# Routing on VectorE in fewer pieces, thresholds as values, and w1 laid out in load order, in an attention and mixture-of-experts kernel

## Chip, cores and metric

The kernel runs on one core of a Trainium2 chip. The metric is the device time of one execution in microseconds (us). Lower is better.

## What is computed

Two layers in one program. The first is an attention with a squared Relu in place of a softmax, over 8 batches of 2496 rows of 256 columns. Its result x, 19968 rows, goes to a mixture of 8 experts with a capacity of 2496 rows each. All (row, expert) pairs are taken in order of falling logit; a row goes to the first expert that still has room. Then each expert's two layers run over its rows.

```python
scores = (1.0 / S) * np.matmul(z, z.transpose(0, 2, 1))
x = (u * np.matmul(np.maximum(scores, 0.0) ** 2, v)).reshape(B * S, D)
logits = x @ w_gate
for idx in np.argsort(-logits.flatten()):
    tok, e = idx // E, idx % E
    if assigned[tok] >= 0 or counts[e] >= cap:   # cap = N // E = 2496
        continue
    assigned[tok] = e
    counts[e] += 1
for e in range(E):
    mask = assigned == e
    out[mask] = np.maximum(x[mask] @ w1[e], 0.0) @ w2[e]   # w1: 256 x 1024, w2: 1024 x 256
```

## The kernel before, in words

**Stages.** Up to about 1358 us the attention runs; all its large matmuls are in pieces of a high and a low part (`hi`, `lo`). Up to about 1423 us there is almost nothing but the routing of the first expert to be filled. From then on the experts run, one after the other, PE nearly always busy, with the routing of the next expert beside them on VectorE (DVE).

**Order of the work.** The attention has an order written out by hand for PE, ScalarE (ACT) and DVE, and so has the first group of the first expert (`first_group`). Everything else is traced in program order and put into each engine's queue by a planner, which uses durations of its own; each engine then works through its queue in order. `advance` mixes the steps of `route(k + 1)` into the loop over expert k, in proportion to the numbers that the generator yields. `behind(lag)` and `issue_after` hold some routing steps behind a step of the expert on the same engine. `warm` puts matmuls without a use into PE's queue while route 0 is alone.

**route(k)** finds the k-th expert that gets full. It has these parts:
- For k > 0 the closed expert is taken out of the logits `lg` (L338), each row's best remaining expert is found by `best_expert` in four quarters of 40 columns (L80 to L97: maximum, comparison, code, one-hot `oh`), and `order_keys` (L108 to L118) turns the maximum into an integer key, a copy `rep` of its upper half eight times over, and `top` and `low`, the halves as floats.
- A search for a threshold in two stages (upper half, lower half), of 5 rounds in route 0 and 6 in the others, each settling 2 to 4 bits. A round makes n = 3, 7 or 15 thresholds `T` from the last digit `Dg` and a prepared row `W` = step + base `V` (L379), compares all keys (`at_least`, L124, `mask`), counts per expert by matmuls (`hist` L281, or `quad_hist` L303 and `quad_sums` L313, L317 in route 0), and takes the largest step that still leaves an expert full (L410, L415). `V` (L394) and the next `W` (L401) are made behind the mask. At the end of a stage `tstar` = `V` + `Dg` (L417).
- Ranks by running sums, and the list: a row's place in its expert's list is split into two digits, one-hot forms of both are made (`oa` L514, `ob` L523 in four pieces for each of four column blocks), `oa` is multiplied by the two halves of the row's number (`hl`, L517), and matmuls add up the list (L529). Route 0 does this in two parts of its own (L541, L554, L559, L564).

**Weights.** `load_w` loads w1 and w2 of the expert in halves, `split_w` makes the high part on ACT (L618) and the low part on DVE (L621). For w1 the source is read with a stride of four elements (L612), for w2 without.

**Experts.** `layer1` makes the first layer for 128 hidden columns and 512 rows (L672 to L674; `hp`, two banks), Relu on ACT (L750, `hh`) and its low part on DVE (L752, `hl_`; L755 for the last 64 rows of an expert). `layer2` (L768, L770) adds up the result three steps behind; `put_y` adds the two halves (L793) and scatters. `gather_x`, `tip_x`, `split_x` fetch and turn the rows of the next group. GpSimd issues gathers and scatters, and prepares `slot` and `hq` (L256, L294) when the attention has ended.

Of the kernel before, what the change touches and what calls it, by code (L numbers as in the profile page):

```python
# [22 lines left out]
def tile_attention_then_moe(ctx, tc, u, ut, v, z, w_gate, gate_rows, w1, w2, out):  # L23
# [36 lines left out]
                 at0=consts.tile([128, 15], I16, name="at0"),  # L60
                 mask0=consts.tile([128, JP, 15], BF, name="mask0"))
    at0_f = consts.tile([128, 15], F32, name="at0_f")
    nc.gpsimd.iota(at0_f, pattern=[[1, 15]], base=1, channel_multiplier=0, allow_small_or_imprecise_dtypes=True)
# [41 lines left out]
def key_steps(nc, first, c, alone):  # L105
# [7 lines left out]
    n = half.shape[1]  # L113
# [22 lines left out]
def moe(tc, xd, first, jp, identf, w1, w2, out, B, S, cp, dram):  # L136
# [19 lines left out]
    ND = 15  # L156
    LA = 3
# [3 lines left out]
    with ExitStack() as ctx:  # L161
# [21 lines left out]
        nc.vector.memset(ones16, 1.0)  # L183
# [27 lines left out]
        need = const([128, E, 16], F16, "need")  # L211
        nc.vector.tensor_scalar(need, dN[:, :, None].to_broadcast([128, E, 16]), float(cap), None, op0=OP.mult)

        floor = const([128, 1], F32, "floor")
        nc.vector.memset(floor, -32768.0)

        def search_plan(i, widths):
            n = max((1 << w) - 1 for w in widths)
            step = const([128, len(widths), n], F32, f"step{i}")
            sh = 16  # L220
            for r, w in enumerate(widths):
# [7 lines left out]
            n = (1 << widths[0]) - 1  # L229
            at0 = const([128, n], I16, f"at0{i}")  # L230
            nc.vector.tensor_scalar(at0, step[:, 0, :n], -32768.0, None, op0=OP.add)
            n = (1 << widths[1]) - 1
            next0 = const([128, n], F32, f"next0{i}")
            nc.vector.tensor_scalar(next0, step[:, 1, :n], -32768.0, None, op0=OP.add)
            return widths, step, at0, next0
# [5 lines left out]
                       base=0, channel_multiplier=1)  # L241
        nc.gpsimd.iota(idi[:TL, B * NT:J], pattern=[[2 * S, B // 2]], base=NT * 128, channel_multiplier=1)
        nc.gpsimd.iota(idi[TL:, B * NT:J], pattern=[[2 * S, B // 2]], base=S + NT * 128, channel_multiplier=1)
# [5 lines left out]
        nc.vector.tensor_scalar(idh_i, idi, 127, None, op0=OP.bitwise_and)  # L249
        nc.vector.tensor_copy(idl, idh_i)  # L250
# [4 lines left out]
        slot = rp.tile([128, 128, QW], BF, name="slot")  # L255
# [19 lines left out]
        nc.vector.tensor_copy(hx, ones_j[:, :1].to_broadcast([128, E * (ND + 1)]).rearrange("p (e t) -> p e t", e=E))  # L275

        def hist(masks, n, order):
            p = srch()
            for c in range(NC):
                lo, of = [s for s in masks if s[0] <= c * 16][-1]  # L280
                latest["mm"] = nc.tensor.matmul(p[:, :n * 16], oh[:, c * 16:(c + 1) * 16].rearrange("p j e -> p (j e)"),  # L281
                                                of(slice(c * 16 - lo, c * 16 - lo + 16)), start=(c == 0),
                                                stop=(c == NC - 1))
# [5 lines left out]
            nc.vector.tensor_mul(hx[:, :, :n], r[:, None, :n].to_broadcast([128, E, n]),  # L289
                                 dE[:, :, None].to_broadcast([128, E, n]))  # L290
            return hx, n + n % 2

        hq = rp.tile([128, 4 * E * (ND + 1)], F16, name="hq")
        nc.gpsimd.tensor_copy(hq, ones_j[:, :1].to_broadcast([128, 4 * E * (ND + 1)]))  # L294

        def quad_hist(of, n, r):
            o = ps.tile([128, 512], F32, name=f"y{r % 2}", bufs=1)[:, :E * (n + n % 2)]
            nc.tensor.matmul(o, ones16, need[:, :, :n + n % 2], start=True, stop=False)
# [9 lines left out]
        def quad_sums(p, o, n, order):  # L308
            nn = n + n % 2
            x = hq[:, :4 * E * nn]  # L310
            v = p[:, :4 * n]
            v = v.rearrange("p (t j) -> p j t", t=n) if order == "tj" else v.rearrange("p (j t) -> p j t", t=n)
            nc.vector.tensor_tensor(x.rearrange("p (j e t) -> p j e t", j=4, e=E)[:, :, :, :n],  # L313
                                    v[:, :, None].to_broadcast([128, 4, E, n]),
                                    own[:, :, :, None].to_broadcast([128, 4, E, n]), op=OP.mult)
            for j in range(4):
                nc.tensor.matmul(o, ones16, x[:, j * E * nn:(j + 1) * E * nn], start=False, stop=(j == 3))  # L317
# [14 lines left out]
        def route(k):  # L332
            if k:
# [29 lines left out]
            else:  # L363
# [6 lines left out]
                widths, step, at0, next0 = plans[k > 0]  # L370
                for stage in range(2):
                    V = floor
                    for r, w in enumerate(widths):
# [6 lines left out]
                        mask = []  # L380
# [4 lines left out]
                        mask.append((0, lambda j, t=whole, n=n: t[:, j, :n]))  # L385
                        yield 2
                        if k:
                            x, nn = hist(mask, n, "jt")
                        else:
                            p, o = quad_hist(mask[0][1], n, r)  # L390
                        warm(k, 4)
                        if r:
# [916 lines left out]
```

## Time and profile before

| | us |
|---|---|
| median of 3 runs | 2431.34 (2430.28 to 2432.57) |
| the profiled execution | 2432.56 |
| its span, first to last instruction | 2430.5 |

| engine | busy us | share | instructions |
|---|---|---|---|
| TensorE (PE), matmuls | 2380.0 | 98% | 14724 |
| VectorE (DVE) | 2068.5 | 85% | 6220 |
| ScalarE (ACT) | 1521.4 | 63% | 2890 |
| GpSimd (POOL) | 460.6 | 19% | 690 |

A share is an average over stages with different limits; what counts for an edit is who is waited for in the stage where it stands. Matmul ends are modelled, and matmuls made by `warm` count as busy. The granted clock is the share of TensorE's full speed that the chip gave.

### The profile page before, as it was taken

What the parts mean: (1) busy time and instruction counts of PE and PEld (TensorE: products, weight loads), DVE (VectorE), ACT (ScalarE), POOL (GpSimd) and SP (SyncE); (2) the same over time, 40 slices, a digit from 0 to 9 for tenths busy, and PEclk for the clock granted to TensorE, in tenths of its full rate; (3) what the DMA queues carried; (4) which work ended last, traced back from release to release, by engine and by line L of the source; (5) the groups of instructions that cost most, each with busy time, mean ns of one, the idle gap of its engine ahead of it and who ended that gap; (6) DMA issues with size and microseconds to landing.
All of it is one profiled execution on the core that took longest, in us unless ns stands there. A gap on an engine that the chain in (4) does not pass through costs nothing.

```text
span 2430.5 us, 42677 instructions
## 1 busy us (share of the span) xinstructions
PE 2380.0 (98%) x14724; PEld 1983.2 (82%) x14724; DVE 2068.5 (85%) x6220; ACT 1521.4 (63%) x2890; POOL 460.6 (19%) x690
## 2 busy tenths in 40 slices
PE   8999999999999999999999999899999999999998
PEld 6888888888888888888887787787888888888887
DVE  7898998998999998989989798979797979797443
ACT  7888888888888988888888223333332333333332
POOL 3020020020010200200100022333233333333332
PEclk9999999999999999999999999999999999999999
DMA  5153261261251532611511023232323323243331
GB/s 154 43 148 86 57 160 43 58 176 53 71 145 44 138 95 57 159 43 53 137 53 43 10 66 118 78 109 80 115 87 95 111 84 118 78 124 119 98 96 57
DMA packets 233848, 222.28 MB, mean 91 GB/s; under 512 B 95392, under 2 KB 192672, under 8 KB 233504
## 3 DMA queue, kind: packets, MB, share of 16 engines
q1 hardware_dynamic: 193088, 150.58, 21.3%
q0 software_dynamic: 40544, 68.98, 10.5%
q8 instruction: 116, 1.90, 0.3%
q14 instruction: 100, 0.82, 0.1%
HBM read 158.67 MB, written 60.82 MB: 90 GB/s over the span
## 4 chain that ended last, share of the span: by engine, by line
PE 82%; DVE 10%; issue 4%; POOL 1%; ACT 1%; DMA 1%; POOLq 0%; DVEq 0%; SPq 0%; ACTq 0%
PE acc L1038 41%; PE sc L996 11%; PE y L768 8%; PE hp L672 4%; PE hp L674 4%; PE hp L673 4%; PE y L770 4%; PE srch L281 2%; PE acc L1043 1%; POOL xg L590 1%; DVE mask L124 1%; DVE ob L523 1%; DVE w1l L621 1%; PE xp L325 1%; PE srch L529 1%
## 5 line engine op out<-in xcount | busy, mean ns | idle before, releaser
L1025 DVE TENSOR_TENSOR lo<-r,hi 128x512 fp32r<-128x512 f32 (+1 forms) x800 | 536.1, 673 | 83.1 <-ACT hi L1017 80.1
L1038 PE MATMUL acc<-hi,vh 128*128 128x512 f32 (+1 forms) x1520 | 590.8, 389 | 0.2 <-ACT vh L970 0.2
L1038 PE MATMUL acc<-lo,vh 128*128 128x512 f32 (+1 forms) x1520 | 587.7, 387 | 2.7 <-DVE lo L1025 2.7
L1038 PE MATMUL acc<-hi,vl 128*128 128x512 f32 (+1 forms) x1520 | 585.9, 385 | 0.0
L750 ACT ACTIVATE hh<-hp 128x512 fp32r<-128x512 f32 (+1 forms) x319 | 187.3, 587 | 629.9 <-PE hp L674 518.4
L1017 ACT ACTIVATE hi<-r 128x512 fp32r<-128x512 f32 (+1 forms) x780 | 500.2, 641 | 122.1 <-ACT r L1012 87.0
L1012 ACT ACTIVATE r<-r 128x512 f32<-128x512 f32 (+1 forms) x800 | 503.6, 639 | 2.5 <-DVE r L1006 2.4
L1079 DVE SCALAR_TENSOR_TENSOR lt<-xs,wgb 128x256 bf16<-128x256 f32 x1192 | 449.2, 417 | 0.0
L768 PE MATMUL y<-w,hh 128*128 128x512 f32 x1216 | 444.8, 399 | 0.7 <-DVE y L793 0.7
L1038 PEld LDWEIGHTS acc<-hi,vh 128*128 128x128 f32 x1520 | 286.2, 188 | 67.0 <-issue 13.8
L1008 ACT ACTIVATE r<-sc 128x512 f32<-128x512 f32 (+1 forms) x638 | 312.4, 614 | 40.3 <-PE sc L996 39.7
L1038 PEld LDWEIGHTS acc<-lo,vh 128*128 128x128 f32 x1520 | 286.3, 188 | 59.2 <-DVE lo L1025 8.2
L1038 PEld LDWEIGHTS acc<-hi,vl 128*128 128x128 f32 x1520 | 286.3, 188 | 52.1
L590 POOL DMA_INDIRECT xg<-xd,idx x160 | 181.2, 1133 | 513.3 <-DVE xg L628 281.1
L768 PEld LDWEIGHTS y<-w,hh 128*128 128x128 f32 x1216 | 229.0, 189 | 49.0 <-DVE y L793 2.2
L672 PE MATMUL hp<-xh,w1h 128*128 128x512 f32 (+2 forms) x642 | 256.5, 400 | 3.6 <-DVE hh L755 2.7
L673 PE MATMUL hp<-xl,w1h 128*128 128x512 f32 (+2 forms) x642 | 252.5, 393 | 1.2 <-DVE xl L666 1.1
L674 PE MATMUL hp<-xh,w1l 128*128 128x512 f32 (+2 forms) x642 | 250.6, 390 | 0.0
L996 PE MATMUL sc<-z,z 64*128 64x512 f32 (+1 forms) x1920 | 236.9, 389 | 4.2 <-ACT z L961 2.8
L996 PEld LDWEIGHTS sc<-z,z 64*128 64x128 f32 x1920 | 200.7, 185 | 31.2 <-ACT z L961 3.5
L959 POOL DMA_DIRECT2D z<-in_z_dram x35 | 18.7, 534 | 960.0 <-DVE lt L1079 530.0
L801 POOL DMA_INDIRECT out_dram<-y,idx x160 | 160.4, 1003 | 207.8 <-DVE y L793 120.9
(1193 smaller groups left out, 3152.1 us busy)
## 6 DMA issues: line engine op xcount, KB each, us to landing
ur<-in_u_dram SPq DMA_DIRECT2D x39, 512.0 KB
flat<-tr SPq DMA_DIRECT2D x152, 128.0 KB
xt<-flat SPq DMA_DIRECT2D x38, 512.0 KB
vh<-in_v_dram POOLq DMA_DIRECT2D x133, 128.0 KB
vr<-in_v_dram SPq DMA_DIRECT2D x32, 512.0 KB
xd<-tr SPq DMA_DIRECT2D x128, 128.0 KB
xs<-xd SPq DMA_DIRECT2D x32, 512.0 KB
wr<-in_moe_w_dram SPq DMA_DIRECT2D x32, 512.0 KB
```

The lines of the kernel that those rows point to most:

```text
L590: return nc.gpsimd.indirect_dma_start(out=dst, out_offset=None, in_=src, in_offset=bass.IndirectOffsetOnAxis(ap=idx, axis=0))
L672: nc.tensor.matmul(p[:, c], wh, xh, start=(d == 0), stop=False)
L673: nc.tensor.matmul(p[:, c], wh, xl, start=False, stop=False)
L674: latest["mm"] = nc.tensor.matmul(p[:, c], wl, xh, start=False, stop=(d == DH - 1))
L768: nc.tensor.matmul(o, h[:, c], w.rearrange("p s d -> p (s d)"), start=(f == 0), stop=(f == FT - 1), skip_group_check=True)
L996: nc.tensor.matmul(pair[s], key[b, p][r, c * 128:c * 128 + 128], query[b, g][r, :w], start=key is ZH and query is ZH, stop=key is ZL)
L1008: recent["r"] = nc.scalar.activation(r, p, AF.Relu, scale=scale)
L1012: nc.scalar.activation(R[n], R[n], AF.Square)
L1017: nc.scalar.activation(h, R[n], AF.Copy)
L1025: recent["l"] = nc.vector.tensor_sub(LO[n], a, h.bitcast(F32))
L1038: nc.tensor.matmul(o[d], w[:, c[d]], x, start=(kt == 0 and i == 0), stop=False)
L1079: nc.vector.scalar_tensor_tensor(t[r], src[r], 1.0, WG["rows"][r, e], op0=OP.mult, op1=OP.mult, accum_out=lg[r, j, e:e + 1])
```

## The change

It does the following.
- Thresholds: counts are scaled by 2^17 (`UNIT`), so that `min(count - capacity, 0) + T` is the threshold itself where an expert is still full and something lower where not. The largest of these is the new base `V`. `T` of the next round is `step + V`, one column wider (its last entry is the base). `W`, `Dg`, `tstar`, `floor` and `next0` go.
- `best_expert` in two halves of 80 columns instead of four quarters.
- `ob` in two pieces for each column block instead of four.
- The rows' numbers are split into 64s and the partition's index instead of 128s and a remainder, in float16 instead of bfloat16; the low part of `hl` is then a product with one scalar per partition, done on ACT.
- `top` and `low` are made on ACT where all keys are made at once (routes 1 to 7).
- w1 is stored in the order in which `split_w` reads it, so that L612's stride is gone.
- GpSimd clears `hq` and the `step` rows (memset); `hx` is cleared on DVE.

```diff
     spread(nc, rep, half[:, :, 1], alone)
     yield
+    if half.shape[1] == first["key"].shape[1]:
+        nc.scalar.activation(top, half[:, :, 1], AF.Copy, scale=65536.0)
+        nc.scalar.activation(low, half[:, :, 0], AF.Copy)
+        return
...
-        idh = const([128, JP], BF, "idh")
-        idl = const([128, JP], BF, "idl")
-        nc.vector.tensor_scalar(idh_i, idi, 7, None, op0=OP.logical_shift_right)
+        idh = const([128, JP], F16, "idh")
+        idl = const([128, JP], F16, "idl")
+        nc.vector.tensor_scalar(idh_i, idi, 6, None, op0=OP.logical_shift_right)
...
-        nc.vector.tensor_copy(idl, idh_i)
+        nc.vector.tensor_copy(idl, pcol.to_broadcast([128, JP]))
...
-        nc.gpsimd.tensor_copy(hq, ones_j[:, :1].to_broadcast([128, 4 * E * (ND + 1)]))
+        nc.gpsimd.memset(hq, 0.0)
...
-                for c in range(0, JP, JP // 4):
-                    eq = rp.tile([128, JP // 4, E], BF, name="eq")
-                    best_expert(nc, first, slice(c, c + JP // 4), eq)
+                for c in range(0, JP, JP // 2):
+                    eq = rp.tile([128, JP // 2, E], BF, name="eq")
+                    for i, _ in enumerate(best_steps(nc, first, slice(c, c + JP // 2), eq)):
+                        if i == 2:
+                            yield 6.8 / 4
                     yield 6.8 / 4
...
-                            T = rp.tile([128, ND], I16, name="T", bufs=2)
-                            nc.vector.tensor_tensor(T[:, :n], W[:, :n], Dg.to_broadcast([128, n]), op=OP.add)
+                            T = rp.tile([128, ND + 1], I16, name="T", bufs=2)[:, :n + 1]
+                            nc.vector.tensor_tensor(T, step[:, r, :n + 1], V.to_broadcast([128, n + 1]), op=OP.add)
...
-                        if r:
-                            V2 = rp.tile([128, 1], F32, name="V", bufs=2)
-                            nc.vector.tensor_tensor(V2, V, Dg, op=OP.add)
-                            V = V2
-                        if r == 0:
-                            W = next0
-                        elif r + 1 < len(widths):
-                            W = rp.tile([128, ND], F32, name="W", bufs=2)
-                            n2 = (1 << widths[r + 1]) - 1
-                            nc.vector.tensor_tensor(W[:, :n2], step[:, r + 1, :n2], V.to_broadcast([128, n2]), op=OP.add)
...
-                                                       o.rearrange("p (e t) -> p e t", e=E)[:, :, :n], 0.0,
-                                                       step[:, r, None, :n].to_broadcast([128, E, n]),
-                                                       op0=OP.is_ge, op1=OP.mult)
-                        Dg = rp.tile([128, 1], F32, name="Dg", bufs=2)
-                        nc.vector.tensor_reduce(Dg, best[:, :, :n], axis=AX.XY, op=OP.max)
-                    tstar = rp.tile([128, 1], F32, name="tstar")
-                    nc.vector.tensor_tensor(tstar, V, Dg, op=OP.add)
+                        best = rp.tile([128, E, ND + 1], F32, name="best")[:, :, :n + 1]
+                        nc.vector.scalar_tensor_tensor(best, o.rearrange("p (e t) -> p e t", e=E), 0.0,
+                                                       T[:, None].to_broadcast([128, E, n + 1]),
+                                                       op0=OP.min, op1=OP.add)
+                        V = rp.tile([128, 1], F32, name="V", bufs=3)
+                        nc.vector.tensor_reduce(V, best, axis=AX.XY, op=OP.max)
+                    tstar = V
...
-                    for i, d in enumerate((idh, idl)):
-                        nc.vector.tensor_mul(hl[:, :, i], oa, by_quad(d[:, q], KT))
+                    nc.vector.tensor_mul(hl[:, :, 0], oa, by_quad(idh[:, q], KT))
+                    nc.scalar.activation(hl[:, :, 1], oa, AF.Copy, scale=pcol)
                     yield 1.5
-                    for b in range(0, 128, 32):
-                        z = b + 32
+                    for b in range(0, 128, 64):
+                        z = b + 64
...
-                        yield 1.5
+                        yield 3
...
-                src = src.rearrange("p (h m q) -> p h q m", h=DH, q=FT // 2)[:, half]
+                src = src.rearrange("p (h q m) -> p h q m", h=DH, q=FT // 2)[:, half]
...
+    w1 = _blocks(inputs['moe_w1'], 1)
+    e, _, f = w1.shape
+    laid['moe_w1'] = w1.reshape(e, d, 2, 128, f // 256).swapaxes(3, 4).reshape(w1.shape)
```

## Rows read from the trace of the kernel before

**Rows 1.** The page, busy time of the engines.

```profile
PE 2380.0 (98%) x14724; PEld 1983.2 (82%) x14724; DVE 2068.5 (85%) x6220; ACT 1521.4 (63%) x2890; POOL 460.6 (19%) x690
```

**Rows 2.** Stretches of 10 us: busy PE, PEld, DVE, ACT, POOL; granted clock, DMA share, GB/s.

```profile
1530.00:1540.00 10.00, 6.25 (x98) 5.25 (x96) 10.00 (x18) 2.34 (x6) 0.00 (x0) 1.00 0.01 2
1540.00:1550.00 10.00, 9.10 (x33) 7.91 (x34) 10.00 (x32) 2.61 (x3) 7.67 (x7) 0.66 0.25 79
...
1680.00:1690.00 10.00, 9.80 (x58) 8.52 (x57) 8.81 (x30) 3.39 (x7) 1.26 (x2) 0.83 0.16 52
...
2060.00:2070.00 10.00, 10.00 (x54) 8.36 (x53) 8.61 (x26) 3.71 (x7) 2.70 (x3) 0.89 0.19 66
```

**Rows 3.** PE's waits, 1500 to 2200 us (last row 1820 to 1945): total, times, longest.

```profile
PE srch L281 <- DVE mask L124: 9.8, 5, 3.3
PE hp L672 <- DVE hh L755: 2.7, 1, 2.7
PE y L770 <- DVE hl__29448 L752: 2.0, 1, 2.0
PE srch L529 <- DVE ob L523: 1.9, 1, 1.9
...
PE srch L281 <- DVE mask L124: 1.9, 1, 1.9
```

**Rows 4.** Timeline of DVE and PE at a first mask: start, us, instruction, idle before.

```profile
1678.35 0.23 DVE L116 TENSOR_SCALAR top<-key 128x160 f32<-128x160 int16 x1
1678.50 0.23 DVE L118 CAST low<-key 128x160 f32<-128x160 int16 x1
...
1680.20 1.09 PE L281 MATMUL srch<-mask,oh 128*128 128x112 bf16 x10 [3.32 <-DVE mask L124]
```

**Rows 5.** DVE's groups by line and shape, from 1420 us: busy us, mean ns of one.

```profile
L523 DVE TENSOR_TENSOR ob<-rab,slot 128x1280 bf16<-128x1280 bf16 x112 | 88.1, 815 | 0.0
L621 DVE TENSOR_TENSOR w1l<-wr,w1h 128x512 fp32r<-128x512 f32 x30 | 32.2, 1079 | 1.0 <-PE hp L674 1.0
L621 DVE TENSOR_TENSOR w<-wr,w 128x512 fp32r<-128x512 f32 x32 | 21.9, 688 | 0.6 <-ACT w L618 0.6
...
L517 DVE TENSOR_TENSOR hl<-oa,idl 128x800 bf16<-128x800 bf16 x28 | 15.8, 566 | 0.0
L514 DVE TENSOR_TENSOR oa<-rab,slot 128x800 bf16<-128x800 bf16 x28 | 15.7, 560 | 0.0
...
L394 DVE TENSOR_TENSOR V<-V,Dg 128x1 f32<-128x1 f32 x48 | 7.3, 153 | 0.0
```

**Rows 6.** Timeline of DVE in the search of route 0.

```profile
1370.25 0.17 DVE L379 TENSOR_TENSOR T<-W,Dg 128x7 int16<-128x7 f32 x1
1370.34 0.15 DVE L394 TENSOR_TENSOR V<-V,Dg 128x1 f32<-128x1 f32 x1
1370.45 0.89 DVE L124 TENSOR_TENSOR mask<-rep,T 128x560 bf16<-128x560 int16 x2
...
1378.61 0.16 DVE L417 TENSOR_TENSOR tstar<-V,Dg 128x1 f32<-128x1 f32 x1
1378.80 0.15 DVE L420 TENSOR_SCALAR base<-tstar 128x1 f32<-128x1 f32 x1
```

**Rows 7.** Timeline of GpSimd and DVE behind the attention, and DVE's same copy later.

```profile
1360.64 0.61 POOL L294 CAST hq<-ones_j 128x512 f16<-128x512 bf16 x1
...
1360.79 0.49 DVE L369 COPY hd<-nrow 128x15 f32<-128x15 f32 x1
...
1449.13 0.18 DVE L369 COPY hd<-nrow 128x15 f32<-128x15 f32 x1
```

**Rows 8.** ACT's groups by line and shape, from 1420 us.

```profile
L618 ACT ACTIVATE w<-wr 128x512 fp32r<-128x512 f32 x28 | 16.1, 623 | 0.7 <-PE y L765 0.7
L132 ACT ACTIVATE rep<-key 128x640 int16<-128x640 int16 x7 | 5.2, 737 | 5.7 <-DVE key L110 5.7
```

**Rows 9.** Timeline of PE at the second group of the first expert.

```profile
1443.66 0.33 PE L642 MATMUL xp<-identf,xg 128*128 128x128 f32 x1 [0.39 <-DMA xg<-xd,idx]
```

More of the change, by code (lines that the diff above doesn't have):

```diff
@@ L210, in moe @@
                                            op0=OP.is_equal, op1=OP.mult)
[L211 to L215, printed above, removed]
+        nc.vector.tensor_scalar(own, own, UNIT / 4096.0, None, op0=OP.mult)
+        need = const([128, E, ND + 1], F16, "need")
+        nc.vector.memset(need, 0.0)
+        nc.vector.tensor_scalar(need[:, :, :ND], dE[:, :, None].to_broadcast([128, E, ND]),
+                                -cap / 16.0 * UNIT / 4096.0, None, op0=OP.mult)
+        dU = const([128, E], F32, "dU")
+        nc.vector.tensor_scalar(dU, dE, UNIT, None, op0=OP.mult)
         def search_plan(i, widths):
-            n = max((1 << w) - 1 for w in widths)
+            n = 1 << max(widths)
             step = const([128, len(widths), n], F32, f"step{i}")
+            nc.gpsimd.memset(step, 0.0)
             sh = 16
@@ L274, in moe, with some, hist @@
         hx = const([128, E, ND + 1], F32R, "hx")
-        nc.vector.tensor_copy(hx, ones_j[:, :1].to_broadcast([128, E * (ND + 1)]).rearrange("p (e t) -> p e t", e=E))
-        def hist(masks, n, order):
+        nc.vector.tensor_scalar(hx, need, 0.0, None, op0=OP.mult)
+        def some(t, n):
+            return t[:, :, ND - n:] if n % 2 else t[:, :, :n]
+        def hist(of, n, order):
             p = srch()
             for c in range(NC):
-                lo, of = [s for s in masks if s[0] <= c * 16][-1]
                 latest["mm"] = nc.tensor.matmul(p[:, :n * 16], oh[:, c * 16:(c + 1) * 16].rearrange("p j e -> p (j e)"),
-                                                of(slice(c * 16 - lo, c * 16 - lo + 16)), start=(c == 0),
-                                                stop=(c == NC - 1))
+                                                of(slice(c * 16, c * 16 + 16)), start=(c == 0), stop=(c == NC - 1))
             v = p[:, :n * 16]
@@ L288, in hist @@
             nc.vector.tensor_reduce(r[:, :n], hd[:, :n], axis=AX.X, op=OP.add)
[L289 to L293, printed above, removed]
-        nc.gpsimd.tensor_copy(hq, ones_j[:, :1].to_broadcast([128, 4 * E * (ND + 1)]))
+            x = some(hx, n)
+            nc.vector.tensor_mul(x[:, :, :n], r[:, None, :n].to_broadcast([128, E, n]),
+                                 dU[:, :, None].to_broadcast([128, E, n]))
+            return x
+        hq = rp.tile([128, 4, E, ND + 1], F16, name="hq")
+        nc.gpsimd.memset(hq, 0.0)
         def quad_hist(of, n, r):
             o = ps.tile([128, 512], F32, name=f"y{r % 2}", bufs=1)[:, :E * (n + n % 2)]
-            nc.tensor.matmul(o, ones16, need[:, :, :n + n % 2], start=True, stop=False)
+            nc.tensor.matmul(o, ones16, some(need, n), start=True, stop=False)
             p = srch()
@@ L434, in route @@
                 if k:
-                    x, nn = hist([(0, lambda j: g[:, :, j])], 2, "tj")
+                    x = hist(lambda j: g[:, :, j], 2, "tj")
                     yield
                     o = srch()[:, :E * 2]
-                    nc.tensor.matmul(o, onesr, x[:, :, :2], start=True, stop=True)
+                    nc.tensor.matmul(o, onesr, x, start=True, stop=True)
                 else:
@@ L1146, in premask @@
         def premask(lo, hi):
-            at_least(nc, first["mask0"], first["rep"], first["at0"], lo, hi)
+            at_least(nc, first["mask0"], first["rep"], first["at0"][:, :15], lo, hi)
         todo, first_in = {}, {}
```

70 lines of the change are left out of this document (30 added, 40 removed).

## Prediction

> **What bounds the kernel now.** I read the page first. TensorE (PE) is busy for 98% of the span [rows 1], so an edit on VectorE (DVE), which is what this change is, can only pay where PE waits for DVE. Busy shares don't say where that is, so the next view was busy time and granted clock in stretches of 10 us. From 1420 us on, where the experts run, PE has 9.2 or more of 10 in all but ten stretches (two of the ten, and two stretches with a lower clock, stand in [rows 2]): the reader is to see PE at 6.25 beside DVE at 10.00, and a granted clock of 0.66 in the stretch behind it. They lie at the change from one expert to the next. The list of PE's waits says for what [rows 3]: the masks of the first search step of a new route (five times, 9.8 us in all: the longest 3.3, then three of 1.9 and one of 0.8), the low part `hh` of an expert's middle layer (2.7), another low part `hl_` (2.0) and the list's one-hot `ob` (1.9). The nine lines of that answer sum to 19.9 us. The timeline shows why: DVE has run without a gap for some 30 us before the mask, through list, weights, best expert and keys, one behind the other, and the L281 matmuls stand at the head of PE's queue for 3.32 us with later work behind them [rows 4].
>
> To this comes the clock. 10 us at a mean of 0.66 have lost 3.4 us (0.34 x 10), a stretch at 0.83 has lost 1.7 and one at 0.89 has lost 1.1 [rows 2]: 6.2 us, through time at the lower level, 1.2 GHz, each right behind a wait. So about 26 us is all that DVE can give back between 1500 and 2200 us. Before that stands the search of route 0, which has no expert work beside it and runs as a chain DVE to PE to DVE of ten rounds; there every DVE step on the chain counts, and PE's busy time is padding (`warm`).
>
> **The change part by part.** The price of one DVE instruction less: 800 elements take 560 ns and 1280 take 815 [rows 5], so 0.53 ns an element and 0.135 us fixed. The next instruction starts 0.15 us after one that lasts 0.23 [rows 4], so 0.08 us of the fixed part overlaps; a fused piece saves about 0.055 us of DVE's time.
>
> Per route from 1 to 7:
> - `ob` in 8 pieces instead of 16: 8 x 0.055 = 0.44 us.
> - the low part of `hl` by ScalarE (ACT): 4 x (0.566 - 0.08) = 1.95 us off DVE [rows 5].
> - best expert in halves instead of quarters, seven instructions each: 14 x 0.055 = 0.77 us.
> - `top` and `low` by ACT: 2 x 0.15 = 0.30 us [rows 4].
> - w1 in the order of its loads: its low part takes 1079 ns where the same operation on the same shape takes 688 for w2 [rows 5]. What differs is that the source is read with a stride of four elements, which the new layout removes: 4 x 0.39 = 1.56 us.
> - thresholds without a base: 10 `V`, 8 `W` and 2 `tstar` go. A `V` lasts 0.15 and the next instruction starts 0.11 after it [rows 5, 6]: 20 x 0.1 = 2.0 us. The result of a round is one column wider, 8 or 16 per expert for 7 or 15, so about 8 ns more in two instructions of 12 rounds: 0.2 us.
>
> Together 6.8 us off DVE in each of the routes 1 to 6, 4.8 in the last, which has no search. Most of it lies beside PE's work and is worth nothing there. What counts is what DVE saves between its last gap and the instruction that PE waits for. Ahead of the 3.3 us wait that is two list pieces (0.98 + 0.17), two w1 halves (0.78), best expert (0.77), `top` and `low` (0.30): 3.0 us. Ahead of each of the three waits of 1.9 us it is 2.5, so all of it; the same for the 2.0 us of `hl_`. Ahead of the stall at 1535 us (1.9 + 2.7) only two list pieces and one w1 half are inside: 0.98 + 0.22 + 0.39 = 1.6. Sum: 1.6 + 3.0 + 5.7 + 2.0 = 12.3 us, if PE's queue stayed as it is.
>
> It will not stay. The order of PE's queue comes from a planner with durations of its own, and it put those matmuls where DVE turned out to be late. What the planner sees of the saving moves the matmul up and keeps the wait; what it does not see goes. The bounds are 0 and 12.3. I take 0.6 of it, because two parts look like the lateness itself: the stride of w1 (0.78; the same shape costs 0.39 less elsewhere) and the fixed part of each instruction (0.94) are 1.72 of the 3.0. So 0.6 x 12.3 = 7.4 us, and of the 6.2 us of clock the same share, 3.7.
>
> Route 0 and its surroundings. `tstar` stands alone on the chain: 0.19 us from its start to that of the next, twice [rows 6], -0.38. `V` costs nothing there: it starts while `T` still runs, and the mask, which needs `T`, starts when `T` has ended (1370.25 + 0.17, against 1370.45) [rows 6]; without `V` the mask still waits for `T`. `W` runs behind the mask, beside PE. The wider result adds 10 x 2 x 0.008 = +0.16. GpSimd clears `hq` instead of copying into it: beside that copy of 0.61 us DVE's `hd` copy takes 0.49 us instead of 0.18 [rows 7], and ends as the other ends, at 1361.25. A clear of this size stands in no row, so between 0 and -0.3; I take half. In the first group w1's low parts lie on DVE's chain and end 0.8 us earlier, but PE waits only 0.39 us for the gather behind them [rows 9]: -0.4. Sum -0.8. The Trainium skill speaks against a larger gain from the clear: SBUF — State Buffer, on the shared port pair, says that a DVE copy in a 2-port mode and a GpSimd operation exclude each other for the whole instruction, also where GpSimd only writes. By it `hd` still ends with the clear, and the term is only what the clear is shorter than 0.61 us; the sum changes by 0.15 us at most.
>
> What is added costs nothing by the same views as long as its cover holds. ACT gets 4 products of 800 elements and two conversions of 160 in a route, and its w1 steps read without the stride too. 640 elements take it 737 ns and 512 take 623 [rows 8], so 800 take about 0.88; ACT is busy for 2.3 to 3.7 of 10 us in the stretches of [rows 2]. The Trainium skill (ScalarE: Activation LUTs, What ACT_TABLE_LOAD costs) adds 93 ns for an operand read per partition, such as the product's scale; no row here has one. By it the product takes 0.97, and the sum is the same. The conversions stand behind ACT's half of `rep`, which waits for the same key, and DVE needs them only six rounds later. No DMA is moved and nothing new is queued on SP. Float16 in place of bfloat16 changes no count of elements. Constants at the start are exchanged about one for one on DVE and GpSimd, where PE waits for loads: bounded by 0.4 us on both sides, taken as 0.
>
> The sum is made against the profiled execution, 2432.6 us with a span of 2430.5; that is 1.2 us above the median of the three runs, 2431.3. 2432.6 - 7.4 - 3.7 - 0.8 = 2420.7.
>
> **The rivals.** (a) Nothing of DVE's relief reaches PE: the planner moves the search matmuls up by as much as DVE gains. For it speaks that the waits come in equal size (1.9) at three changes of expert, so they belong to the plan and not to chance; against it that two parts of the saving look like lateness. Only -0.8 is left: 2431.8, or about 2429 with one dip of the clock gone.
> (b) All goes: DVE's whole 12.3, the 6.2 of clock and the 0.8: 2413.3, and with the small waits, up to 3 us, 2410. For it: DVE's saving covers the wait at four of six places and nearly at a fifth. Against it: at 1535 us it covers a third.
> (c) Slower: ACT now stands in the list's chain. It works in order, so where a product is queued ahead of an expert's Relu (L750) and its `oa` is not written, the Relu waits, the low part on DVE waits for the Relu, and PE, which has two `hp` banks, waits for both (this is the 2.7 us wait of [rows 3]). Price: up to 0.88 us at each of 28 list pieces, 24.6 us, against 11.9 gained: 2445.3. It turns the sign from about half of the pieces on. For it: DVE is late against the plan in just these stretches. Against it: ACT is idle for two thirds of them, and behind 1560 us PE never waits for the list.
> (d) The new layout does not shorten the w1 steps, say because the write is what is slow. Then 0.4 us are missing ahead of the stall at 1535, 0.8 ahead of the 3.3, 0.2 at each 1.9 and 0.3 at the 2.0: 0.6 x 2.1 = 1.3 us, 2422. It stays inside the forecast.
>
> **How the numbers follow.** Forecast with (d), a gain of 6 to 17 us, 2421: 0.55. (b) 0.12. (a) 0.20. (c) 0.13. A measurement of this kernel can tell about 0.2%, 4.9 us, from no change, so faster is below 2426.5: 0.55 + 0.12 = 0.67; within: 0.20; slower: 0.13. The range from 2408 to 2433 holds the forecast, (a) and (b), and leaves out (c).
>
> **What would show it.** In the changed kernel's profile: the list's one-hot 56 times at about 1.5 us; w1's low part at 0.69 us; DVE with about 330 instructions fewer and 45 to 65 us less busy; ACT with 42 more. Right: PE's waits for masks from 9.8 to about 4 us, the stall at 1535 us still there with 3 us, and one of the three dips of the clock left at most. Wrong by (a): the same masks waited for as long as before though w1 is faster. Wrong by (b): no wait over 1 us. Wrong by (c): PE waits for `hh` or `hl_`, and ACT's Relu stands behind a product that waits for DVE's `oa`. The prediction also fails if a new order of the queue puts a wait of some 3 us, with the clock behind it, where there is none now.

## The result and the profile after

The changed kernel takes 2405.57 us (median of four, 2404.27 to 2406.74) beside 2430.81 for the kernel before (four, 2429.59 to 2432.57): a ratio of 0.9891, 95% interval 0.9878 to 0.9905. That is 25.2 us faster, where the forecast was 11.9 with a range that ended at 2408. The profiled execution took 2404.67 us with a span of 2402.8. The two profiled executions are 27.9 us apart (27.7 by their spans), 2.6 more than the medians: the one of before lies 1.75 above its median and the one of after 0.9 below.

The page's first lines, which answer [rows 1]:

```profile
PE 2367.3 (99%) x14724; PEld 1975.7 (82%) x14724; DVE 2023.1 (84%) x5887; ACT 1533.2 (64%) x2932; POOL 473.2 (20%) x693
```

DVE has 333 instructions fewer and is 45 us less busy, ACT has 42 more, as the prediction said. PE is 12.7 us less busy with the same number of matmuls. About 10 us of that are the clock: summed over stretches of 10 us up to the end of the last expert, the granted clock lost 13.6 us before and 3.4 now. The rest fits matmuls that overlap less around a wait, which is taken up below. The stretches that answer [rows 2], in the columns given there:

```profile
1530.00:1540.00 10.00, 7.79 (x72) 6.83 (x71) 10.00 (x25) 2.43 (x5) 4.97 (x6) 1.00 0.18 54
1540.00:1550.00 10.00, 8.01 (x47) 6.39 (x47) 9.91 (x29) 3.86 (x8) 3.68 (x4) 1.00 0.47 129
1660.00:1670.00 10.00, 9.41 (x49) 8.11 (x48) 9.99 (x30) 4.63 (x11) 4.04 (x4) 1.00 0.34 89
2030.00:2040.00 10.00, 10.00 (x61) 8.75 (x60) 9.45 (x28) 4.81 (x10) 4.04 (x4) 1.00 0.45 111
```

The granted clock is 1.00 in all of them. Between 1420 and 2390 us no stretch shows a lower one, where before lost 6.2 us by [rows 2], and 6.8 with one smaller dip. That is one execution, with a mean granted clock of 0.997; the other three have 0.995 to 0.997. PE's waits from 1500 to 2175 us, all that the view lists, for [rows 3]:

```profile
PE hp L664 <- DVE hh L747: 2.2, 1, 2.2
PE y L762 <- DVE hl__20924 L744: 1.3, 1, 1.3
PE srch L288 <- issue: 1.1, 1, 1.1
PE y L762 <- DVE hl__20881 L744: 0.7, 1, 0.7
PE hp L664 <- ACT hh L742: 0.6, 1, 0.6
PE hp L665 <- DVE xl L658: 0.5, 1, 0.5
PE srch L430 <- DVE hx L296: 0.3, 1, 0.3
```

6.7 us in place of 19.9. Four of the rows (5.3 us) belong to the first change of expert, at 1532 to 1556 us; from 1700 to 2160 us the view lists no wait of PE. A first mask now, from the timeline (for [rows 4]):

```profile
1790.91 0.33 ACT L117 ACTIVATE top<-key 128x160 f32<-128x160 int16 x1
1791.14 0.33 ACT L118 ACTIVATE low<-key 128x160 f32<-128x160 int16 x1
1791.48 0.83 DVE L128 TENSOR_TENSOR mask<-rep,at 128x1120 bf16<-128x1120 int16 x1
1792.36 0.65 PE L288 MATMUL srch<-mask,oh 128*128 128x112 bf16 x10
```

`top` and `low` are on ACT, and the matmul behind the mask has no wait in brackets.

What the work costs, by line and shape (busy us, mean ns of one), for [rows 5, 8]; the last row is of the kernel before:

```profile
L515 DVE TENSOR_TENSOR ob<-rab,slot 128x2560 f16<-128x2560 f16 x56 | 82.7, 1479 | 0.0
L613 DVE TENSOR_TENSOR w1l<-wr,w1h 128x512 fp32r<-128x512 f32 x32 | 21.7, 682 | 0.5 <-PE hp L666 0.5
L509 ACT ACTIVATE hl<-oa,pcol 128x800 f16<-128x800 f16 x28 | 26.9, 960 | 19.4 <-PE srch L521 8.9 <-DVE oa L506 8.4 <-DVE hl__29295 L744 2.0
L610 ACT ACTIVATE w1h<-wr 128x512 fp32r<-128x512 f32 x28 | 16.8, 624 | 16.2 <-PE hp L665 13.5 <-issue 1.5 <-DMA wr<-in_moe_w_dram 1.2
```
```profile
L618 ACT ACTIVATE w1h<-wr 128x512 fp32r<-128x512 f32 x28 | 30.4, 1125 | 18.5 <-PE hp L673 17.8 <-DMA wr<-in_moe_w_dram 0.7
```

The one-hot in two pieces takes 1479 ns (forecast about 1.5 us), w1's low part 682 (0.69), so rival (d) is out. ACT's part of w1 gains more than DVE's: 1125 to 624 ns.

### The profile page after: what moved, and what is told of

The parts are those of the page before. It is cut to its first block, busy times and chain, and to the rows that moved or that the text cites. A ratio compares the mean times of both kernels' runs of the same rounds, so it can differ in the third digit from the quotient of the medians.

```text
span 2402.8 us, 42417 instructions
## 1 busy us (share of the span) xinstructions
PE 2367.3 (99%) x14724; PEld 1975.7 (82%) x14724; DVE 2023.1 (84%) x5887; ACT 1533.2 (64%) x2932; POOL 473.2 (20%) x693
## 4 chain that ended last, share of the span: by engine, by line
PE 87%; issue 4%; DVE 4%; POOL 1%; ACT 1%; DMA 1%; SPq 0%; POOLq 0%; DVEq 0%; ACTq 0%
PE acc L1030 41%; PE sc L988 11%; PE y L760 10%; PE hp L664 5%; PE hp L665 5%; PE hp L666 5%; PE y L762 5%; PE acc L1035 1%; PE srch L288 1%; PE srch L521 1%; POOL xg L582 1%; PE xp L330 1%; DVE lo L1017 1%; POOL out_dram L793 1%; DVE mask L128 1%
## 5 line engine op out<-in xcount | busy, mean ns | idle before, releaser
L582 POOL DMA_INDIRECT xg<-xd,idx x160 | 188.0, 1175 | 478.6 <-DVE xg L620 252.7
L664 PE MATMUL hp<-xh,w1h 128*128 128x512 f32 (+2 forms) x642 | 254.6, 398 | 2.8 <-DVE hh L747 2.2
L793 POOL DMA_INDIRECT out_dram<-y,idx x160 | 165.9, 1037 | 204.5 <-DVE y L785 107.3
```

Source lines behind the costliest of these rows:

```text
L582: return nc.gpsimd.indirect_dma_start(out=dst, out_offset=None, in_=src, in_offset=bass.IndirectOffsetOnAxis(ap=idx, axis=0))
L664: nc.tensor.matmul(p[:, c], wh, xh, start=(d == 0), stop=False)
```

## The experiments

Three batches, each beside its own runs of the kernel before (medians 2432.18, 2429.21 and 2429.11). "Place" is the number of the experts' matmuls (hp and y) that stand ahead of a route's first mask matmul in PE's queue, counted in the instruction order of the compiled kernels (the traces show the same numbers):

| kernel | route 1 | 2 | 3 | 4 | 5 | 6 |
|---|---|---|---|---|---|---|
| before, only_w1, only_thr | 211 | 613 | 1139 | 1691 | 2243 | 2795 |
| only_list | 211 | 613 | 1139 | 1697 | 2249 | 2801 |
| only_best | 205 | 615 | 1150 | 1699 | 2251 | 2803 |
| place_alone | 209 | 617 | 1149 | 1701 | 2253 | 2805 |
| after, no_w1, no_thr | 205 | 614 | 1147 | 1695 | 2247 | 2799 |
| load_alone | 199 | 614 | 1141 | 1691 | 2243 | 2795 |
| place_early | 196 | 608 | 1124 | 1671 | 2223 | 2775 |
| no_best | 209 | 613 | 1139 | 1698 | 2250 | 2802 |
| no_list, low_on_dve | 205 | 614 | 1151 | 1701 | 2253 | 2805 |

The wait of 3.3 us [rows 3, 4] belongs to route 3, the three of 1.9 to routes 4 to 6. (The expectations that speak of it as the second route's count one short. Their 12.4 and 4.3 us for the halves and for w1 alone are 12.7 and 4.2 by the medians given here.)

Two rows of the table bear on the prediction by themselves: taking 1.6 us (w1) or 1.8 us (thresholds) a route off DVE moved none of the first masks. They moved only where pieces were merged and the numbers that the routing yields changed with them.

To compare kernels I read PE's waits from 1700 to 2120 us, where three changes of expert follow each other that are alike. Before has these two rows there, 6.2 us; after has none:

```profile
PE srch L281 <- DVE mask L124: 5.7, 3, 1.9
PE y L768 <- DVE y L793: 0.5, 3, 0.2
```

**One part alone: w1.**

```diff
-                src = src.rearrange("p (h m q) -> p h q m", h=DH, q=FT // 2)[:, half]
+                src = src.rearrange("p (h q m) -> p h q m", h=DH, q=FT // 2)[:, half]
...
+    laid['moe_w1'] = w1.reshape(e, d, 2, 128, f // 256).swapaxes(3, 4).reshape(w1.shape)
```

> The kernel before with w1 alone in the order of its loads. The queues of all five engines are the same as before, instruction by instruction, so the planner takes nothing back. Full theory (what DVE saves ahead of a wait reaches PE in full): two low parts of w1 end 0.78 us earlier ahead of each first-mask wait (3.3 and three times 1.9), about as much ahead of the 2.0 us wait for hl_, 0.39 ahead of the stall at 1535 us, 0.4 at the gather of the second group: 4.7 us, and up to 2 us of clock: 2424 to 2426.5. Rival (the gain of the whole change is the new order of PE's queue and not DVE's load): 2430 to 2432. w1l falls from 1079 to about 690 ns, w1h from 1125 to about 625 ns under both.

2427.97 us, ratio 0.9982 (0.9972 to 0.9991): a gain of 4.2 us, between the two ranges. In the same stretch the masks are still waited for:

```profile
PE srch L281 <- DVE mask L124: 5.6, 3, 1.9
```

The longest, 3.3 at route 3, is 2.7 now. Of the 0.78 us that DVE saves ahead of each mask 0.6 arrived at one. At the others the mask's wait fell by less than 0.1, and the wait of 0.2 for `y` beside it went, so about 0.25 in all. DVE has a gap there that it did not have before, 0.22 us ahead of a low part:

```profile
1788.07 0.56 DVE L752 SCALAR_TENSOR_TENSOR hl__24250<-hp,hh 128x384 fp32r<-128x384 f32 x1 [0.22 <-issue]
```

**Best expert in halves alone.**

```diff
-                for c in range(0, JP, JP // 4):
-                    eq = rp.tile([128, JP // 4, E], BF, name="eq")
-                    best_expert(nc, first, slice(c, c + JP // 4), eq)
+                for c in range(0, JP, JP // 2):
+                    eq = rp.tile([128, JP // 2, E], BF, name="eq")
+                    for i, _ in enumerate(best_steps(nc, first, slice(c, c + JP // 2), eq)):
+                        if i == 2:
+                            yield 6.8 / 4
                     yield 6.8 / 4
```

> The kernel before with best_expert in halves alone. The planner puts the first masks of the routes from 3 on 8 to 11 expert matmuls later in PE's queue (about 0.24 us each, so 2 to 2.6 us), that of route 2 two later. Queue theory: the waits of 1.9 us go for that reason alone, the 3.3 us wait falls by 0.5, and DVE's 0.77 us ahead of each comes on top: 6 to 9 us, 2422 to 2425. Load theory (only what DVE does less counts): 5 x 0.77 = 3.9 us, 2427.

2419.53 us, ratio 0.9949 (0.9932 to 0.9965): 12.7 us for 0.77 us of DVE's work a route, more than either theory gave. No mask is waited for at these three changes; something else is:

```profile
PE hp L674 <- DVE hh L757: 4.9, 3, 1.6
```

From route 2 on the first masks stand 2, 11, 8, 8 and 8 matmuls later in PE's queue.

**The list alone** (one-hot in two pieces, low part on ACT, float16).

```diff
-                    for i, d in enumerate((idh, idl)):
-                        nc.vector.tensor_mul(hl[:, :, i], oa, by_quad(d[:, q], KT))
+                    nc.vector.tensor_mul(hl[:, :, 0], oa, by_quad(idh[:, q], KT))
+                    nc.scalar.activation(hl[:, :, 1], oa, AF.Copy, scale=pcol)
...
-                    for b in range(0, 128, 32):
-                        z = b + 32
+                    for b in range(0, 128, 64):
+                        z = b + 64
```

> The kernel before with the list's change alone (float16, numbers as 64s and partition, low part of hl by ACT, one-hot in two pieces). Load theory: DVE saves 1.2 us ahead of the 3.3 us wait, 0.7 ahead of the three waits of 1.9, 1.2 to 2.4 ahead of the stall at 1535: 4.5 to 6 us and some clock: 2424 to 2427. Rival that ACT's product holds up the Relu of the expert: 2433 or more, with PE waits for hh or hl_ between 1500 and 2200 us that were not there. The product itself takes about 0.88 us by the nearest rows, 0.97 by the Trainium skill (ScalarE: Activation LUTs, What ACT_TABLE_LOAD costs).

2422.35 us, ratio 0.9957 (0.9941 to 0.9974): 9.8 us, and below the load theory's range. At these three changes no first mask is waited for. What PE waits for stands later in the search, `hx` and the mask of a later round:

```profile
PE srch L405 <- DVE hx L289: 4.4, 6, 1.1
PE srch L281 <- DVE mask L124: 1.7, 3, 0.7
```

The wait of 1.9 us for `ob` at 1535 us is gone. ACT's products hold up no Relu that PE waits for, which was rival (c); once, at 1633 us, PE waits 0.4 us for `xh`, which stands on ACT behind a product.

**The thresholds alone** (no V, W, tstar; counts scaled by 2^17).

```diff
-                            T = rp.tile([128, ND], I16, name="T", bufs=2)
-                            nc.vector.tensor_tensor(T[:, :n], W[:, :n], Dg.to_broadcast([128, n]), op=OP.add)
+                            T = rp.tile([128, ND + 1], I16, name="T", bufs=2)[:, :n + 1]
+                            nc.vector.tensor_tensor(T, step[:, r, :n + 1], V.to_broadcast([128, n + 1]), op=OP.add)
...
```

> The kernel before with the thresholds alone (20 small DVE instructions less in each route, hq cleared). PE's queue stays within two matmuls of the one before. Load theory: none of this lies between DVE's last gap and a first mask, so only route 0 gains, 0.4 us, and nothing beside the experts: 2430 to 2431. Rival (DVE's total load counts, wherever it is taken off, 2 us a route): 2425 or less.

2433.12 us, ratio 1.0005 (0.9995 to 1.0015): 1.8 us a route less on DVE are worth nothing, and the masks' row is that of before:

```profile
PE srch L285 <- DVE mask L125: 5.7, 3, 1.9
```

So the halves give more than DVE saves by them, and the thresholds nothing for more DVE time saved. The place in the queue was a candidate, and the next two kernels part it from the load. (Both change only the order in which the routing's steps are mixed into the expert's, so DVE's own order moves with PE's.)

**The place alone.**

```diff
-                for c in range(0, JP, JP // 4):
-                    eq = rp.tile([128, JP // 4, E], BF, name="eq")
-                    best_expert(nc, first, slice(c, c + JP // 4), eq)
+                for c in range(0, JP, JP // 2):
+                    eqs = [rp.tile([128, JP // 4, E], BF, name="eq", bufs=2) for _ in range(2)]
+                    both = [best_steps(nc, first, slice(c + i * JP // 4, c + (i + 1) * JP // 4), eqs[i]) for i in range(2)]
+                    for i, _ in enumerate(zip(*both)):
+                        if i == 2:
+                            yield 6.8 / 4
+                    for t in both:
+                        for _ in t:
+                            pass
                     yield 6.8 / 4
```

> The kernel before with its four quarters of best expert kept, all 28 instructions of them, but taken two and two together, so that the numbers which the loop yields come at the places where the halves yield them. DVE does the same work as before; in PE's queue the matmuls that read a route's first mask now stand behind 617, 1149, 1701, 2253 and 2805 matmuls of the experts instead of 613, 1139, 1691, 2243 and 2795 (counted from the first expert on), so 4 and then four times 10 later, at 0.24 us each 1.0 and 2.4 us. Two theories. By the place in the queue: the three waits of 1.9 us go though DVE saves nothing, the one of 3.3 shrinks to about 2.3, most of the clock comes back, 2419 to 2423, much like the halves alone (2419.5). By the load: what counts is what DVE saves, and it saves nothing, so the waits for masks stay at 9.8 us in all and the time at 2430 to 2434.

2421.02 us, ratio 0.9969 (0.9956 to 0.9981). DVE saves nothing, and 8.2 us go. At the three changes the masks' waits are gone, others stand in their place, 3.4 us for 6.2:

```profile
PE hp L678 <- DVE eq L91: 2.1, 3, 0.7
PE y L774 <- DVE y L799: 1.3, 3, 0.4
```

(`eq` is no operand of that matmul; the view names the DVE instruction that came last.) At the first change of expert it lost: the wait for `hh` there is 4.1 us, 2.7 before [rows 3].

**The load alone**: the changed kernel with the masks at the old places.

```diff
                         if i == 2:
-                            yield 6.8 / 4
-                    yield 6.8 / 4
+                            yield 6.0 / 4
+                    yield 6.0 / 4
```

> The changed kernel with 6.0 in place of 6.8 in the two numbers that its halves of best expert yield. No instruction of any engine differs, only their order: the first masks' matmuls stand behind 614, 1141, 1691, 2243 and 2795 matmuls of the experts, against 614, 1147, 1695, 2247 and 2799 in the changed kernel and 613, 1139, 1691, 2243 and 2795 in the kernel before, so at the old places. By the place in the queue: the three waits return with about 1.0 to 1.9 us each and the clock with them, 2411 to 2417. By the load: DVE has saved 2.5 us ahead of each wait of 1.9, so none returns and the time stays at 2405 to 2408.

2405.49 us, ratio 0.9898 (0.9881 to 0.9914): as the changed kernel. With the masks back at the places where PE waited 1.9 us for them, PE waits once in the three changes. DVE's own order did not help: by the trace, ahead of each of these masks stand one `hl_` and one piece of weights more than in the kernel before.

```profile
PE srch L430 <- DVE hx L296: 0.3, 1, 0.3
```

**The same yields, smaller still.**

```diff
-                            yield 6.8 / 4
-                    yield 6.8 / 4
+                            yield 5.0 / 4
+                    yield 5.0 / 4
```

> The changed kernel with 5.0 in place of 6.8 in the numbers that its halves of best expert yield: the same instructions, the first masks' matmuls 6, 23 and three times 24 matmuls of the experts earlier in PE's queue than in the changed kernel, that is 16 to 20 earlier than in the kernel before for four routes, 3.8 to 4.8 us. It asks how much cover DVE's saving has left. If place counts beside load, waits for masks of 2 to 4 us return four times, with the clock, 2415 to 2423. If DVE's own steps move up with the masks and DVE has time to spare ahead of them, 2405 to 2408.

2420.11 us, ratio 0.9967 (0.9955 to 0.9978): 14.5 us lost to the changed kernel with not one instruction other than its. The time lies in the first theory's range, but by luck: no mask is waited for. PE waits for the next group's rows instead:

```profile
PE hp L665 <- DVE xl L658: 2.7, 3, 0.9
PE hp L664 <- ACT xh L657: 2.2, 3, 0.7
```

```profile
1756.53 0.95 ACT L509 ACTIVATE hl<-oa,pcol 128x800 f16<-128x800 f16 x1
...
1757.65 1.15 ACT L657 ACTIVATE xh<-xt 128x512 fp32r<-128x512 f32 x2
...
1758.33 0.73 PE L664 MATMUL hp<-xh,w1h 128*128 128x512 f32 x2 [0.74 <-ACT xh L657]
...
1759.21 1.29 DVE L658 TENSOR_TENSOR xl<-xt,xh 128x512 fp32r<-128x512 f32 x2
...
1759.95 0.50 PE L665 MATMUL hp<-xl,w1h 128*128 128x512 f32 x1 [0.89 <-DVE xl L658]
```

`xh` stands on ACT behind four pieces of `y` with the list's product among them, and `xl` on DVE behind `oa` and w1l: the planner's new order, not the amount of work, puts them late. Dips of the clock come with it, 6.8 us between 1550 and 2150 us.

**One part left out.** The changed kernel with one part as it was; the diffs are those above, turned round.

> The changed kernel with best expert in four quarters as before. First masks behind 613, 1139, 1698, 2250 and 2802 matmuls, so at the old places for two routes and 7 later for the other three. By the place: waits return at the first two, about 2 to 3.3 and 1.9 us with a clock dip behind each, and at no other, 2411 to 2416. By the load: the 0.77 us that halves save are missing ahead of each wait, of 2.5 to 3.0 saved in all, so waits of 1.1 at the first and 0.2 at the others, 2406 to 2409. Going by the sum of single parts (the halves alone gave 12.4 us) it would be 2417 to 2419.

2406.97 us, ratio 0.9907 (0.9890 to 0.9923). The halves, worth 12.7 us alone, are worth 1.4 to 3 here. Waits for masks of 1.1 and 1.0 us are left at routes 2 and 3, and there is none from 1700 to 2120.

> The changed kernel with the list as before: one-hot in four pieces for each block, low part by DVE, bfloat16. First masks behind 614, 1151, 1701, 2253 and 2805 matmuls, so 1, 12 and three times 10 later than before. The wait for the list's one-hot at 1535 us returns with about 1.9 us and a clock dip of up to 3 behind it. By the place: only that and part of the 3.3 at the second route's mask, 2411 to 2415. By the load: the list is the largest part of what DVE saves (2.4 of 6.8 us a route), so without it the waits for masks return in part, about 1 us each, 2414 to 2419.

2413.05 us, ratio 0.9929 (0.9913 to 0.9946). The `ob` wait of 1.9 us is back at 1534 us, from route 3 on the masks stand 10 to 12 matmuls later than before, and DVE's lateness shows at `hh`, not at the masks as the load theory had it:

```profile
PE hp L664 <- DVE hh L747: 2.5, 3, 0.8
```

> The changed kernel with w1 in its old layout; the queues of all engines are those of the changed kernel, and DVE's w1 pieces take 1.08 us again instead of 0.68, ACT's 1.13 instead of 0.62. By the cover (several parts each hide the same waits, and one can be missing): as without the halves of best expert, small waits of up to 1 us at the first masks of routes 1 and 2 and at the stall at 1535 us, 2406 to 2409. By the sum of single parts: w1 alone gave 4.3 us, so 2409 to 2411.

2411.64 us, ratio 0.9928 (0.9911 to 0.9945): 6.1 us, more than the 4.2 that w1 gave alone, so the expectation of a replaceable part was wrong here. `hx` is waited for in the search, and `hh` at 1535 us for 2.6 us.

```profile
PE srch L399 <- DVE hx L296: 1.1, 3, 0.4
```

> The changed kernel with thresholds, counts and the row's numbers in their old form (a running base, W and Dg), all else as changed. Alone the new thresholds gave nothing (2433.1 against 2432.2). If they stand on no path here either, 2405 to 2407. If the 2.0 us a route that they take off DVE help once the larger waits are gone, PE waits inside the search, for hx or for the masks of later rounds, 0.2 us here and there: 2407 to 2411.

2406.11 us, ratio 0.9905 (0.9888 to 0.9921): no difference that these runs can tell, and waits as in the changed kernel, each within 0.1 us. The thresholds are worth nothing alone and nothing behind the others.

**The low part back on DVE**, all else as changed.

```diff
-                    nc.scalar.activation(hl[:, :, 1], oa, AF.Copy, scale=pcol)
+                    nc.vector.tensor_mul(hl[:, :, 1], oa, by_quad(idl[:, q], KT))
```

> The changed kernel with the low part of hl made by DVE again (28 products of about 0.57 us, 1.95 us a route beyond the overlap), the one-hot in two pieces as changed. The first masks stand 4 to 6 matmuls later in PE's queue than in the changed kernel. Leaving out the whole change of the list cost 7.5 us; ACT's product is 1.95 of the 2.4 us that it saves a route. By the load: four fifths of it, 2410 to 2413, with the stall at 1535 us longer by about 1 us. By the place: the later masks hide it and only the stall grows, 2406 to 2408.

2411.49 us, ratio 0.9924 (0.9907 to 0.9941). ACT's product is 5.9 of the list's 7.5 us; DVE's lateness shows at `hh` again:

```profile
PE hp L664 <- DVE hh L747: 1.6, 3, 0.5
```

What each part was worth, alone and as the last one:

| part | DVE us a route, estimated | alone, us | as the last, us |
|---|---|---|---|
| list | 2.4 | 9.8 | 7.5 |
| w1 | 1.6 | 4.2 | 6.1 |
| best expert | 0.8 | 12.7 | 1.4 |
| thresholds | 1.8 | -0.9 | 0.5 |

("Alone" is against the median of its batch's kernel before, "as the last" against 2405.57, which is of another batch; measured from each batch's own kernel before, every figure of the last column is 1.6 to 1.7 us larger, so its order holds, and 1.4 is not clear of nothing. `top` and `low` were not tried by themselves.) No kernel beat the changed one: the best of them, 2405.49, is the same within what can be measured.

## Why the prediction was wrong

**Right.** Where the time lay: in PE's waits for DVE at the changes of expert and in the clock behind them. The prices of the edited instructions: the one-hot, w1 and the product on ACT. Both zeros: the thresholds, and what ACT takes over. Rival (c) does not show in the changed kernel: its one wait for ACT, 0.6 us for a Relu at 1662 us, has no product ahead of it. What shows elsewhere is PE waiting for `xh`, not for a Relu, behind a product on ACT: four times 0.7 us between 1750 and 2140 us in place_early, once 0.4 to 0.5 in only_list and in no_w1, and once 1.0 in load_alone:

```profile
2169.03 0.96 ACT L509 ACTIVATE hl<-oa,pcol 128x800 f16<-128x800 f16 x1 [1.74 <-DVE oa L506]
...
2171.18 1.14 ACT L657 ACTIVATE xh<-xt 128x512 fp32r<-128x512 f32 x2
```

The Trainium skill (ScalarE: Activation LUTs, What ACT_TABLE_LOAD costs) has 93 ns for an operand read per partition. The trace agrees: 160 elements take ACT 326 ns without that operand, in the row below, and 640 took 737 [rows 8], so 800 would take 0.87 us; the product takes 0.96.

```profile
L117 ACT ACTIVATE top<-key 128x160 f32<-128x160 int16 x7 | 2.3, 326 | 0.0
```

**Route 0**, forecast -0.4. Each `tstar` was worth what was said: from the last `T` to `base` 2.98 us before (1375.82 to 1378.80), 2.80 now; a round takes 2.80, 2.79 before, so `V` and `W` did stand beside the chain. Over all of route 0 the two profiles differ by 0.6 us: 0.4 of that lies in the first round, 3.19 us before and 2.80 now, which no term of the sum foresaw; why is open.

```profile
1373.57 0.17 DVE L385 TENSOR_TENSOR T<-step,V 128x8 int16<-128x8 f32 x1
...
1376.11 0.22 DVE L408 TENSOR_REDUCE V<-best 128x1 f32<-128x64 f32 x1
1376.37 0.15 DVE L412 TENSOR_SCALAR base<-V 128x1 f32<-128x1 f32 x1
```

The clear of `hq` gained 0.04 us, not 0.15 (0.57 us for the 0.61 of [rows 7]). DVE's copy still ends with it, at 1359.43 and 1359.40. The Trainium skill (SBUF — State Buffer, Terms, the shared port pair) says that of the two engines the one that loses the pair is blocked for the other's full instruction. The trace agrees:

```profile
1358.83 0.57 POOL L301 MEMSET hq<- 128x512 f16 x1
1358.98 0.45 DVE L376 COPY hd<-nrow 128x15 f32<-128x15 f32 x1
```

**The step that failed is the factor of 0.6.** The prediction held that the planner takes back part of DVE's saving by moving the masks' matmuls up. The compiled order shows the reverse: the five masks that PE waited for moved down, by 1, 8, 4, 4 and 4 matmuls (only route 1's, which it did not wait for, moved up). In the kernels with w1 or the thresholds alone DVE saves 1.6 and 1.8 us a route and no first mask moves at all. And moving down was not needed: the load alone, with these masks at or near the old places, removes the waits just as well. So nothing was taken back, at either place. Without the factor the prediction's own sum is rival (b), 2413.3, and with the small waits 2410, which was given a chance of 0.12. (Its own sign, no wait over 1 us, did not come: 2.2, 1.3 and 1.1 us are left at the first change of expert.) Two parts of the argument misled: that 1.72 of the 3.0 us "look like lateness" is no reason why the rest should be taken back, and the order of the queue, which is fixed when the kernel is compiled, was argued about and not bounded by what a change of place would cost.

**What was missing beyond (b).** Each expert ends with 448-wide matmuls. Measured from one expert's first and last of these (of L672 before, L664 after) to the next's, the profiled executions differ by 25.2 us behind route 0. At full worth the terms are 18.9 with the 0.4 of the first group. The first change of expert (4.7 against 5.0 with its clock) and the second (4.3 against 4.7) came out as summed, the first in part by luck: the wait for `ob` went whole, and two new ones for `hl_` (0.7 and 1.3) came. Too small were:
- the three waits of 1.9, summed at 5.7 with 1.1 of clock, measured 9.2 over the three stretches (2.6, 2.5 and, with the clock's dip, 4.1), and the 2.0 of `hl_`, measured 2.7. One of the three before, and then the same after, from the first 448-wide matmul of an expert to its last one of L672 (L664 after), in the columns of [rows 2]:

```profile
1790.95:1812.65 21.70, 19.58 (x109) 16.97 (x108) 21.70 (x70) 8.87 (x16) 7.82 (x8) 1.00 0.34 97
```
```profile
1778.05:1797.15 19.10, 19.10 (x109) 16.90 (x108) 18.44 (x53) 8.32 (x18) 5.87 (x6) 1.00 0.37 104
```

The same 109 matmuls take 2.6 us less, of which 2.1 were idle; 0.5 were in PE's busy time at a full clock. Matmuls overlap: one that lasts 0.37 starts 0.21 after its predecessor in the timeline of before. A wait breaks the overlap, which costs these 0.16 us beside the idle time; with two waits in the stretch (1.9 and 0.2) that is 0.3 of the 0.5, and the rest is not shown.

```profile
1791.15 0.37 PE L673 MATMUL hp<-xl,w1h 128*128 128x448 f32 x1
1791.36 0.37 PE L674 MATMUL hp<-xh,w1l 128*128 128x448 f32 x1
```

- waits under 1 us, with what goes with them: 1.6 in the first group (the gather's 0.39 of [rows 9] and two for `hx`) and 1.7 beside the last route (1.5 listed). To this come 1.0 net in the stretches between the changes, from -0.7 to +0.5 each, which the listed waits do not account for. The prediction gave the first 0.4 and the others nothing.

That is 3.1 and 3.9 us too little, and 0.7 too much at the first two changes: the 6.3 by which 25.2 exceeds 18.9.

**How the parts work together.** A wait is what DVE is late by, less the work that stands ahead of the waiting matmul. The halves alone acted mostly by their place: nearly the same place without the saving gives 8.2 us of the 12.7. But a later place does not pay what DVE owes; PE then waits for `hh` (only_best 1.6, no_list 0.8, low_on_dve 0.5 at each change). Only less work on DVE in these stretches ends that: list and w1 are the parts that nothing replaces. In the whole change the halves' part is hidden behind theirs. The 1.8 us of the thresholds are spread over the search, behind the masks that were waited for; the prediction left them out of its 12.3, rightly.

**Left open.** The stall at 1535 us remains with 4.2 us (2.2, 0.7 and 1.3), where 3 were foretold. In the attention both kernels' PE waits 2.7 us for the same low part, with a clock dip behind it in some profiled executions (3.4 us in the one of before, none in the one of after, 0 to 1.7 in the twelve experiments); it is not put down to the change, and probably makes up part of the 2.6 us by which the profiles are further apart than the medians: ahead of route 0 they already differ by 1.8 us (1360.64 of [rows 7] against 1358.83). Why w1 is worth more as the last part than alone was not tried further; the gap on DVE in w1 alone is a candidate.

## What to carry to other kernels

A discount for a planner that may take a saving back needs a reason of its own, and the order that it compiles shows whether the waiting matmul moves up, down or not at all. Sum a saving over all the waits that it shortens, the small ones and the broken overlap included, and take the clock behind each along; then ask which other part of the change would have removed the same wait. A later place hides a late engine at one point and shows it at the next; less work on the engine is what ends it.

## What the runs showed of the hardware

- A wait of PE costs more than the view shows: 1.9 us listed, with 0.2 beside it, were 2.6 in the stretch. Matmuls of 0.37 us start 0.21 apart, and behind a wait that overlap starts anew, which accounts for 0.3 of the 0.5.
- Reading with a stride of four elements costs ACT more than DVE: for 512 elements 1125 against 624 ns on ACT, 1079 against 682 on DVE.
- With the same instructions on every engine, two numbers that set only the order were worth 14.5 us (5.0 against 6.8), and between 6.0 and 6.8 nothing.
